# Loading queries and keys 20 steps ahead of their pair instead of 11, in a bucketed attention kernel with a routed expert layer

## The chip, the core and the metric

The kernel runs on one core of one Trainium2 chip. TensorE (PE, with its weight loads shown apart as PEld), VectorE (DVE), ScalarE (ACT) and GpSimd (POOL) compute; SyncE (SP) issues nearly all the DMAs and computes nothing. The metric is the device time of one execution in microseconds, as the median of several runs. A profiled execution gives the span between its first and last instruction, and the trace that is read here.

## What is computed

There are 4 batches of 8 heads, 768 positions of 64 numbers each, and then 8 experts over 3072 tokens of 512 numbers. Cut to what matters:

```python
q_bits = (q @ proj > 0);  k_bits = (k @ proj > 0)          # 6 bits for each position and head
mask = bucket(q_bits)[:, None] == bucket(k_bits)[None, :]
scores = where(mask, q @ k.T / 8, -1e9)
attn = exp(scores - max); attn /= attn.sum() + 1e-9
x = (attn @ v) laid out as 3072 tokens x 512
e = argmax(x @ w_gate);  out = gate * eom * (relu(x @ w1[e]) @ w2[e])
```

## The kernel before

The attention half goes over 16 pairs of heads (`g` from 0 to 15). A pair is 12 steps of scores, 192 steps in all, and a step is one tile of 128 queries against 768 keys for one head. The kernel writes out by hand what PE, DVE, ACT and POOL do in each step, in program order, so these four follow the code. SP is not among them: its DMAs are put in order by the framework that builds the program, which starts from the step where they stand in the code, and SP then works through that order, waiting at each DMA until its source is there and its target free.

Within a step `s`: `scores(s)` multiplies on PE (L533) and DVE copies the result with the mask's limit and the minimum (L537); `soft` is the exponential on ACT (L545); `normal` scales two steps' rows by their reciprocal sums on POOL (L555); `transposed(s - 6)` turns the tile of six steps earlier on PE (L566), and ACT copies it out (L567). At every sixth step from step 12 on there is a longer block: under "matmuls" stands `weighted`, 12 products with the values of six steps (24 matmuls of PE, L577).

What the change touches is how a pair is made ready:

- `load(g)`, L393 to L399: two DMAs of 384 KB, one for each head, bring queries and keys into tiles `qk`. There are 4 such tiles, so pair `g` takes those of pair `g - 2`.
- `project(g)`, L405 to L416: 8 small matmuls (L411), four for each head, and one DVE operation (L414) give the sign bits `bt` of the hash.
- `split_hi` and `split_lo`, L485 to L500: POOL and DVE make two float32r parts of `qk`, in tiles `xl` and `yl`.
- `spread(g, j)`, L502 to L516: for each head 8 DMAs of SP from one place of the on-chip memory to another put these parts and the bits into the form that `scores` reads.
- `load_v(g)` (L401 to L403) brings the values of a pair, `rows` (L582 to L596) writes a finished pair to memory in four DMAs.

The loop over `g` near L721 gives these functions their steps. With `s0 = 12 * (g - 1)`, which is the first step of the pair before, the kernel has: `load(g)` at step `s0 - 11`, at the end of it; `project(g)` in the block of step `s0 - 6`, behind `weighted`; splits and spreads of pair `g` in the block of step `s0`. Scores of pair `g` begin at step `s0 + 12`. `plan(step, fn)` puts a function at the end of a step, `block(step, when, fn)` at a named place inside a long block. Loads of pairs 0 and 1 stand ahead of the loop over steps, and pair 1 has steps of its own.

After the attention follow the routing of tokens to experts and the expert layer, whose weights are loaded by SP as well. None of their code is touched.

Of the kernel before, what the change touches and what calls it, by code (L numbers as in the profile page):

```python
# [45 lines left out]
PER = 6  # L46
# [13 lines left out]
def lsh_attention_then_moe(  # L60
# [307 lines left out]
    with ExitStack() as actx:  # L368
# [16 lines left out]
        def plan(step, *fns):  # L385
            at.setdefault(step, []).extend(fns)

        def block(step, when, *fns):

            around.setdefault((step, when), []).extend(fns)  # L390


        def load(g, heads=(0, 1)):  # L393
            st = pairs[g]
            st.setdefault("qk", [])
            for j in heads:
                t = hp.tile([P, S], F32, name="qk", bufs=4)
                nc.sync.dma_start(t, qkT[2 * g + j])
                st["qk"].append(t)  # L399

        def load_v(g):  # L401
            pairs[g]["v"] = tp.tile([P, 2, NT, D], F32, name="vt", bufs=2)
            nc.sync.dma_start(pairs[g]["v"], v[g])  # L403

        def project(g):  # L405
            st = pairs[g]
            pp = ps_m.tile([P, HS], F32, name="ps_m")
            for j in range(2):
                for n in range(2):
                    r = 32 * (2 * j + n)  # L410
                    nc.tensor.matmul(pp[r:r + 32], pjc, st["qk"][j][:, n * HS:(n + 1) * HS],  # L411
                                     start=True, stop=True)
            bt = hp.tile([P, HS], F32R, name="bt", bufs=2)
            nc.vector.tensor_scalar(bt, pp, thr, scl, ALU.is_gt, ALU.mult)  # L414
            st["bt"] = bt
# [69 lines left out]
        def split_hi(g, j, xl=None):  # L485
            st = pairs[g]
            for k in ("xl", "yl", "xr", "yr"):
                st.setdefault(k, [None, None])
            if xl is None:
                xl = hp.tile([P, S], F32R, name="xl")  # L490
            nc.gpsimd.tensor_scalar(xl, st["qk"][j], sgn, 0.0, ALU.mult, ALU.add)
            st["xl"][j] = xl

        def split_lo(g, j, n):
            st = pairs[g]
            if n == 0:
                st["yl"][j] = hp.tile([P, S], F32R, name="yl")
            cs = slice(n * HS, (n + 1) * HS)
            nc.vector.scalar_tensor_tensor(st["yl"][j][:, cs], st["qk"][j][:, cs], sgn, f32(st["xl"][j][:, cs]),
                                           ALU.mult, ALU.subtract)  # L500

        def spread(g, j):  # L502
            st = pairs[g]
            xl, yl, bt = f32(st["xl"][j]), f32(st["yl"][j]), f32(st["bt"])
            st["xr"][j] = hp.tile([P, S], F32R, name="xr")
            st["yr"][j] = hp.tile([D + 2 * NB, S], F32R, name="yr")
            xr, yr = f32(st["xr"][j]), f32(st["yr"][j])
            nc.sync.dma_start(xr[0:D], xl[D:P])
            nc.sync.dma_start(yr[0:D], xl[D:P])
            nc.sync.dma_start(xr[D:P], yl[D:P])  # L510
            nc.sync.dma_start(xl[D:P], xl[0:D])
            for n in range(2):
                r = 32 * (2 * j + n)
                cs = slice(n * HS, (n + 1) * HS)
                nc.sync.dma_start(yr[D:D + 2 * NB, cs], bt[r + 2 * NB:r + 4 * NB])
                nc.sync.dma_start(yl[D:D + 2 * NB, cs], bt[r:r + 2 * NB])  # L516
# [52 lines left out]
        def weighted(hb, c):  # L569
            g, hf = hb // 2, hb % 2  # L570
            st = pairs[g]
            if c == 0:
                st["av"] = ps_a.tile([P, HS], F32, name="ps_a")
            if c == NT - 1 and hf == 0:
                st["ot"] = gp.tile([P, S], F32, name="ot", bufs=4)
            for j in range(2):
                nc.tensor.matmul(st["av"][j * D:(j + 1) * D], st["v"][:, j, c], blocks[hb][j][:, c],  # L577
                                 start=(c == 0), stop=(c == NT - 1))
            if c == NT - 1:
                nc.vector.tensor_copy(st["ot"][:, hf * HS:(hf + 1) * HS], st["av"])  # L580

        def rows(g, hf, whole=True):  # L582

            b, i = divmod(g, H // 2)
            st = pairs[g]
            if hf == 0:
                st["xb"] = gp.tile([P, S // 32, 32], F32, name="xb", bufs=2)
            ts = slice(hf * HS // 32, (hf + 1) * HS // 32)
            nc.vector.transpose(st["xb"][:, ts].rearrange("p n c -> p (n c)"), st["ot"][:, hf * HS:(hf + 1) * HS])
            if whole:  # L590
                if hf == 0:
                    return
                ts = slice(0, S // 32)
            xv = x_dram[b * S:(b + 1) * S].rearrange("(n r) c -> r n c", r=32)
            for a in range(4):
                nc.sync.dma_start(xv[:, ts, i * P + 32 * a:i * P + 32 * (a + 1)], st["xb"][32 * a:32 * (a + 1), ts])  # L596
# [124 lines left out]
        for g in range(NP):  # L721
            s0 = 12 * (g - 1)
            if g >= 2:
                plan(s0 - 11, lambda g=g: load(g))
                block(s0 - PER, "matmuls", lambda g=g: project(g))
                block(s0, "head", *(lambda g=g, j=j: split_hi(g, j) for j in range(2)))
                block(s0, "early", lambda g=g: split_lo(g, 0, 0))
                block(s0, "amid", lambda g=g: split_lo(g, 0, 1), lambda g=g: split_lo(g, 1, 0))
                block(s0, "behind", lambda g=g: split_lo(g, 1, 1), *(lambda g=g, j=j: spread(g, j) for j in range(2)))
            elif g == 1:  # L730
                plan(4, lambda: project(1))
                for j in range(2):
                    plan(2 + j, lambda j=j: split_hi(1, j))
                    for n in range(2):
                        plan(3 + 2 * j + n, lambda j=j, n=n: split_lo(1, j, n))
                    plan(5 + j, lambda j=j: spread(1, j))
            if g >= 1:
                plan(s0 + 10, lambda g=g: load_v(g))
            for hf in range(2 if g + 1 < NP else 1):
                block(12 * g + 6 * hf + 2 * PER, "matmuls", *(  # L740
                    lambda hb=2 * g + hf, c=c: weighted(hb, c) for c in range(NT)))
                if g + 1 < NP:
                    plan(12 * g + 6 * hf + 2 * PER, lambda g=g, hf=hf: rows(g, hf))
        for i, fn in enumerate(more_constants()):
            plan(18 + 2 * i, fn)
        for b in range(B - 1):
            r = routing(b)
            s0 = 12 * (H // 2) * (b + 1)
# [10 lines left out]
        s0 = 12 * (NP - 1)  # L759
# [415 lines left out]
```

## Time and profile before

| | us |
|---|---|
| median of 3 runs | 780.19 (777.91 to 780.93) |
| the profiled execution | 777.2 |
| its span, first to last instruction | 775.5 |
| PE busy | 750.9, 97% of the span |
| DVE, ACT, POOL busy | 483.2, 460.9, 387.7 |
| PE idle in 0 to 530 us while waiting for `qk` | 7.8 in 9 waits |

The profiled execution is the one that all rows come from, so sums are made against its own 777.2. Matmuls overlap on PE: a timeline row's duration may reach into the next row, and what a group of matmuls costs is best read as the distance from its start to the start of the group behind it. A step of the attention half is some 2.2 us long on average, a pair some 26 us.

### The profile page before, as it was taken

To read this page: it belongs to the slowest core of one execution; us is meant where nothing else is said; L and a number is where in the kernel's file an instruction comes from. 1 tells how busy PE (TensorE), PEld (TensorE's weight loads), DVE (VectorE), ACT (ScalarE), POOL (GpSimd) and SP (SyncE) were. 2 spreads that over 40 slices of the span, in tenths; PEclk is the share of its full clock that TensorE was granted. 3 is DMA by queue.
4 is the path that set the end of the run, shared out by engine and by line. 5 is a ranking of instruction groups with operands and counts; after the bars stand their busy time and mean duration, and the time that the engine had idled before them with its cause. 6 is when DMAs were issued, how large, how long until landed. Compare 5 with 4: busy or idle time off the path is not lost. (4 is left out here: it accounts for less than half of the span.)

```text
span 775.5 us, 13677 instructions
## 1 busy us (share of the span) xinstructions
PE 750.9 (97%) x4690; PEld 607.9 (78%) x4690; DVE 483.2 (62%) x1032; ACT 460.9 (59%) x934; POOL 387.7 (50%) x422
## 2 busy tenths in 40 slices
PE   7899989999999999999999999999999999999997
PEld 5667766867767677686778768988999999989895
DVE  5757756788766787676798727246263635455540
ACT  5768868778777877788787841243342534353331
POOL 7545635445553554555357893453537363736201
PEclk9999999999999999999999999999999999999999
DMA  4564464555455555554545332363444444446501
GB/s 169 116 173 98 88 167 110 107 132 135 99 140 116 108 128 121 141 116 106 117 89 151 77 93 68 122 214 118 144 153 155 152 150 155 151 151 218 195 18 39
DMA packets 84799, 98.89 MB, mean 128 GB/s; under 512 B 57999, under 2 KB 59439, under 8 KB 84720
## 3 DMA queue, kind: packets, MB, share of 16 engines
q1 hardware_dynamic: 79376, 84.58, 42.2%
q0 software_dynamic: 5200, 13.31, 5.1%
q8 instruction: 40, 0.66, 0.3%
q14 instruction: 39, 0.32, 0.1%
q10 hardware_dynamic: 144, 0.02, 0.0%
HBM read 59.49 MB, written 13.11 MB: 94 GB/s over the span
## 5 line engine op out<-in xcount | busy, mean ns | idle before, releaser
L555 POOL TENSOR_SCALAR sc<-sc,rsum 128x768 f32<-128x768 f32 x192 | 185.9, 982 | 202.7 <-DVE rsum L553 99.4
L567 ACT COPY pts<-ps_t 128x384 f32<-128x384 f32 x384 | 165.1, 483 | 93.4 <-PE ps_t L566 92.4
L537 DVE TENSOR_SCALAR_CACHE_REDUCE sc<-ps_s 128x768 f32<-128x768 f32 x192 | 182.6, 954 | 55.7 <-PE ps_s L533 53.0
L545 ACT ACTIVATE sc<-sc,mn 128x768 f32<-128x768 f32 x192 | 178.2, 935 | 7.7 <-DVE sc L537 7.7
L566 PE MATMUL ps_t<-ident,sc 128*128 128x128 f32 x1152 | 160.7, 275 | 3.3 <-ACT pts L567 2.9
L566 PEld LDWEIGHTS ps_t<-ident,sc 128*128 128x128 f32 x1152 | 133.5, 141 | 33.5 <-POOL sc L555 16.2
L577 PE MATMUL ps_a<-pts,vt 128*64 128x384 f32 x768 | 131.1, 491 | 0.0
L533 PE MATMUL ps_s<-xr,xl 128*128 128x384 f32 x384 | 115.3, 382 | 3.6 <-POOL xl L481 2.2
L577 PEld LDWEIGHTS ps_a<-pts,vt 128*64 128x64 f32 x768 | 52.2, 137 | 67.7 <-issue 67.5
L323 DVE SCALAR_TENSOR_TENSOR hl<-ps_s,hh 128x256 fp32r<-128x256 f32 (+8 forms) x40 | 34.0, 849 | 108.0 <-ACT hh L322 108.0
L533 PE MATMUL ps_s<-yr,yl 76*128 76x384 f32 x384 | 99.8, 341 | 0.6 <-POOL yr L443 0.5
L312 PE MATMUL ps_s<-xh,w1h 128*128 128x256 f32 (+7 forms) x288 | 97.1, 337 | 1.7 <-DVE eq L647 1.6
L312 PE MATMUL ps_s<-xlo,w1h 128*128 128x256 f32 (+7 forms) x288 | 95.4, 331 | 0.0
L312 PE MATMUL ps_s<-xh,w1l 128*128 128x256 f32 (+7 forms) x288 | 95.2, 331 | 0.0
L286 POOL DMA_INDIRECT xq<-x_dram,idx x75 | 82.7, 1102 | 23.7 <-issue 20.8
L329 POOL DMA_INDIRECT out_dram<-yo,sid x29 | 30.6, 1056 | 115.8 <-ACT yo L328 63.9
L322 ACT ACTIVATE hh<-ps_s 128x256 fp32r<-128x256 f32 (+8 forms) x40 | 29.0, 726 | 96.6 <-PE ps_s L312 96.6
L533 PEld LDWEIGHTS ps_s<-yr,yl 76*128 76x128 f32 x384 | 70.5, 191 | 1.2 <-POOL yr L443 1.2
L533 PEld LDWEIGHTS ps_s<-xr,xl 128*128 128x128 f32 x384 | 58.7, 193 | 6.5 <-POOL xl L481 2.5
L312 PEld LDWEIGHTS ps_s<-xh,w1h 128*128 128x128 f32 x288 | 54.2, 188 | 3.8 <-issue 2.4
L312 PEld LDWEIGHTS ps_s<-xlo,w1h 128*128 128x128 f32 x288 | 54.2, 188 | 1.3 <-DVE xlo L269 0.2
L312 PEld LDWEIGHTS ps_s<-xh,w1l 128*128 128x128 f32 x288 | 54.1, 188 | 1.1
(204 smaller groups left out, 1024.4 us busy)
## 6 DMA issues: line engine op xcount, KB each, us to landing
w_raw<-in_w_dram SPq DMA_DIRECT2D x36, 512.0 KB
qk<-in_qkT_dram SPq DMA_DIRECT2D x32, 384.0 KB
xh<-in_w_dram SPq DMA_DIRECT2D x14, 512.0 KB
xlo<-in_w_dram SPq DMA_DIRECT2D x14, 512.0 KB
vt<-in_v_dram SPq DMA_DIRECT2D x16, 384.0 KB
xr<-xl SPq DMA_DIRECT2D x30, 192.0 KB
yr<-xl SPq DMA_DIRECT2D x30, 192.0 KB
xr<-yl SPq DMA_DIRECT2D x30, 192.0 KB
```

What stands on the lines that cost most here:

```text
L286: nc.gpsimd.indirect_dma_start(out=xq[:, k * P:(k + 1) * P], out_offset=None, in_=x_dram.rearrange("n (a f) -> (n a) f", a=NB32), in_offse ...
L312: nc.tensor.matmul(ps, l, r, start=first and k == 0, stop=last and k == len(pairs) - 1)
L322: nc.scalar.activation(hh, ph, AF.Relu)
L323: return lambda: nc.vector.scalar_tensor_tensor(hl, ph, 0.0, f32(hh), ALU.max, ALU.subtract)
L329: nc.gpsimd.indirect_dma_start(out=out[:, :], out_offset=bass.IndirectOffsetOnAxis(ap=sid[0:n, r, a:a + 1], axis=0), in_=yo[0:n], in_offse ...
L533: nc.tensor.matmul(ss[:, n, 0:HS], l[0:k, qs], r[0:k, n * HS:(n + 1) * HS], start=first, stop=not first)
L537: nc.vector.tensor_scalar(sc, ss[:, :, 0:HS], MASKED, None, ALU.min, ALU.min, accum_out=mn)
L545: nc.scalar.activation(pr, pr, AF.Exp, bias=mn, scale=-1.0, accum_out=sums[s // GROUP][:, k:k + 1])
L555: nc.gpsimd.tensor_scalar(live[s0 + k], live[s0 + k], rs[:, k:k + 1], 0.0, ALU.mult, ALU.add)
L566: nc.tensor.transpose(tr[:, c], pr[:, (3 * h + c) * P:(3 * h + c + 1) * P], ident)
L567: nc.scalar.copy(pts[:, 3 * h:3 * h + 3, t * P:(t + 1) * P], tr)
L577: nc.tensor.matmul(st["av"][j * D:(j + 1) * D], st["v"][:, j, c], blocks[hb][j][:, c], start=(c == 0), stop=(c == NT - 1))
```

## The change

Three numbers change in the loop that gives the steps. From pair 3 on, `load(g)` stands at step `s0 - 20`, not `s0 - 11`, which is four steps behind the block in which pair `g - 2` is split and spread (for pair 3 at step 8, not 13). For pair 2 the load stays at step 1, and its projection goes from the block of step 6 to the end of step 10. Nothing is added or taken away.

```diff
             if g >= 2:
-                plan(s0 - 11, lambda g=g: load(g))
-                block(s0 - PER, "matmuls", lambda g=g: project(g))
+                plan(max(s0 - 20, 8) if g > 2 else 1, lambda g=g: load(g))
+                if g > 2:
+                    block(s0 - PER, "matmuls", lambda g=g: project(g))
+                else:
+                    plan(10, lambda g=g: project(g))
                 block(s0, "head", *(lambda g=g, j=j: split_hi(g, j) for j in range(2)))
```

On SP, the stretch between the spreads of two pairs, before. The first row is the last DMA of the spread of pair 4; `qk_1264` and `qk_1266` are pair 5, `qk_1605` and `qk_1607` pair 6; the last row opens the spread of pair 5:

```order
L516 DMA yl_1180<-bt_1027 12x384
L398 DMA qk_1264<-in_qkT_dram 128x768
L398 DMA qk_1266<-in_qkT_dram 128x768
L403 DMA vt_1484<-in_v_dram 128x768
L398 DMA qk_1605<-in_qkT_dram 128x768
L398 DMA qk_1607<-in_qkT_dram 128x768
L596 DMA x_dram_63<-xb_1239 32x24x32 x4
L508 DMA xr_1551<-xl_1512 64x768
```

The same stretch now. The first row is again the last DMA of the spread of pair 4, `qk_1327` and `qk_1329` are pair 6, and the last row opens the spread of pair 5:

```order
L516 DMA yl_1184<-bt_1031 12x384
L398 DMA qk_1327<-in_qkT_dram 128x768
L398 DMA qk_1329<-in_qkT_dram 128x768
L596 DMA x_dram_63<-xb_1243 32x24x32 x4
L403 DMA vt_1488<-in_v_dram 128x768
L508 DMA xr_1555<-xl_1516 64x768
```

Pair 5's loads have moved ahead of the spread of pair 4, out of this stretch; what stands behind that spread is the load of pair 6 alone, and the values now come behind the rows that are written out. Before, such stretches held by turns anything from no load to four (two pairs' worth); now each holds one pair's two.

On SP near the start, before, around the spread of pair 2 (it runs from `xr_495` to the last `bt_326`; `qk_549` and `qk_551` are pair 3):

```order
L516 DMA yl_305<-bt_283 12x384
L508 DMA xr_495<-xl_456 64x768
L509 DMA yr_496<-xl_456 64x768
L510 DMA xr_495<-yl_463 64x768
...
L516 DMA yl_470<-bt_326 12x384
L398 DMA qk_549<-in_qkT_dram 128x768
L398 DMA qk_551<-in_qkT_dram 128x768
```

And now (`qk_381` and `qk_383` are pair 3, `qk_612` pair 4):

```order
L516 DMA yl_305<-bt_283 12x384
L398 DMA qk_381<-in_qkT_dram 128x768
L398 DMA qk_383<-in_qkT_dram 128x768
L508 DMA xr_499<-xl_460 64x768
L509 DMA yr_500<-xl_460 64x768
...
L516 DMA yl_474<-bt_432 12x384
L398 DMA qk_612<-in_qkT_dram 128x768
```

Pair 3's load stood behind the spread of pair 2 and now stands ahead of it.

On PE the only move is pair 2's projection. Before, at step 6 (`sc_198` is the tile of step 0):

```order
L411 MATMUL ps_m_321<-qk_225,pjc_66 32x384 x2
L411 MATMUL ps_m_321<-qk_227,pjc_66 32x384 x2
L566 MATMUL ps_t_330<-ident_68,sc_198 128x128 x3
L566 MATMUL ps_t_335<-ident_68,sc_198 128x128 x3
L533 MATMUL ps_s_351<-xr_154,xl_150 128x384 x2
```

And now, at the end of step 10 (`sc_269` is the tile of step 4):

```order
L566 MATMUL ps_t_415<-ident_68,sc_269 128x128 x3
L566 MATMUL ps_t_420<-ident_68,sc_269 128x128 x3
L411 MATMUL ps_m_427<-qk_225,pjc_66 32x384 x2
L411 MATMUL ps_m_427<-qk_227,pjc_66 32x384 x2
L533 MATMUL ps_s_434<-xr_154,xl_150 128x384 x2
```

The 8 matmuls (a row counts a pair of them as one) stand four steps later, and the DVE operation L414 on their result moves with them. Every other instruction of PE, DVE, ACT and POOL keeps its place.

## Rows read from the trace of the kernel before

**Rows 1.** The page: busy time by engine, and the clock that TensorE was granted in 40 slices of the span (9 is nine tenths or more of full speed).

```profile
PE 750.9 (97%) x4690; PEld 607.9 (78%) x4690; DVE 483.2 (62%) x1032; ACT 460.9 (59%) x934; POOL 387.7 (50%) x422
...
PEclk9999999999999999999999999999999999999999
```

**Rows 2.** Who waited for whom, of PE alone, from 0 to 530 us: microseconds in total, times, longest.

```profile
PE ps_m L411 <- DMA qk<-in_qkT_dram: 7.8, 9, 1.7
PE ps_t L566 <- ACT pts L567: 2.9, 4, 1.9
```

**Rows 3.** Timeline of PE around the projection of pair 5: start, duration, and in brackets the idle time ahead of it with what ended that.

```profile
100.66 4.09 PE L577 MATMUL ps_a<-pts,vt 128*64 128x384 f32 x24
106.50 0.84 PE L411 MATMUL ps_m<-qk,pjc 128*32 128x384 f32 x4 [1.75 <-DMA qk<-in_qkT_dram]
108.38 0.84 PE L411 MATMUL ps_m<-qk,pjc 128*32 128x384 f32 x4 [1.04 <-DMA qk<-in_qkT_dram]
109.15 0.88 PE L566 MATMUL ps_t<-ident,sc 128*128 128x128 f32 x6
...
116.72 0.60 PE L533 MATMUL ps_s<-xr,xl 128*128 128x384 f32 x2
```

**Rows 4.** Timeline of PE around the projection of pair 4.

```profile
74.93 4.09 PE L577 MATMUL ps_a<-pts,vt 128*64 128x384 f32 x24
78.95 0.85 PE L411 MATMUL ps_m<-qk,pjc 128*32 128x384 f32 x8
79.73 0.88 PE L566 MATMUL ps_t<-ident,sc 128*128 128x128 f32 x6
```

**Rows 5.** Timeline of PE around the projections of pairs 3, 7, 9, 11, 13 and 15, two rows for each: for pair 3 the group ahead of the projection and the one behind it, for the others the first half of the projection and the group behind its second half.

```profile
46.41 4.09 PE L577 MATMUL ps_a<-pts,vt 128*64 128x384 f32 x24
...
54.03 0.87 PE L566 MATMUL ps_t<-ident,sc 128*128 128x128 f32 x6
...
161.74 0.84 PE L411 MATMUL ps_m<-qk,pjc 128*32 128x384 f32 x4
...
163.55 0.87 PE L566 MATMUL ps_t<-ident,sc 128*128 128x128 f32 x6
...
215.86 0.84 PE L411 MATMUL ps_m<-qk,pjc 128*32 128x384 f32 x4
...
218.60 0.87 PE L566 MATMUL ps_t<-ident,sc 128*128 128x128 f32 x6
...
271.18 0.84 PE L411 MATMUL ps_m<-qk,pjc 128*32 128x384 f32 x4
...
273.06 0.88 PE L566 MATMUL ps_t<-ident,sc 128*128 128x128 f32 x6
...
325.40 0.84 PE L411 MATMUL ps_m<-qk,pjc 128*32 128x384 f32 x4
...
327.87 0.88 PE L566 MATMUL ps_t<-ident,sc 128*128 128x128 f32 x6
...
380.46 0.84 PE L411 MATMUL ps_m<-qk,pjc 128*32 128x384 f32 x4
...
382.66 0.87 PE L566 MATMUL ps_t<-ident,sc 128*128 128x128 f32 x6
```

**Rows 6.** Timeline of SP's DMA queue: when the DMA instructions were issued. The row at 48.15 is the last of the spread of pair 2, the one at 53.36 the load of pair 4; the one at 103.07, right behind the spread of pair 4, is the load of pair 5, and the one at 105.16 that of pair 6.

```profile
48.15 0.71 SPq L516 DMA_DIRECT2D yl<-bt  x1
...
53.36 0.98 SPq L398 DMA_DIRECT2D qk<-in_qkT_dram  x2
...
103.07 0.98 SPq L398 DMA_DIRECT2D qk<-in_qkT_dram  x2
...
105.16 0.91 SPq L398 DMA_DIRECT2D qk<-in_qkT_dram  x2
110.46 2.13 SPq L596 DMA_DIRECT2D x_dram<-xb  x4
```

**Rows 7.** Busy time of each engine in three stretches: length, busy time and instructions of PE, PEld, DVE, ACT and POOL, granted clock of PE, DMA share and GB/s. The first runs from the end of `weighted` to the transposes behind the projection of pair 5, the other two are the 12 steps behind it and the 12 behind those (each up to the end of the next projection, without its wait).

```profile
104.68:109.15 4.47, 1.68 (x11) 0.29 (x9) 0.77 (x3) 0.50 (x2) 1.91 (x3) 1.00 0.87 280
...
109.15:135.64 26.49, 26.49 (x186) 19.24 (x184) 18.71 (x45) 21.50 (x49) 12.67 (x14) 1.00 0.52 119
135.64:162.52 26.88, 26.88 (x190) 19.91 (x186) 20.76 (x56) 21.78 (x51) 12.46 (x13) 1.00 0.54 117
```

**Rows 8.** Timeline of POOL in the block of pair 5's projection: the scalings whose results the transposes behind it read.

```profile
103.02 1.78 POOL L555 TENSOR_SCALAR sc<-sc,rsum 128x768 f32<-128x768 f32 x2 [3.24 <-DVE rsum L553]
105.22 1.78 POOL L555 TENSOR_SCALAR sc<-sc,rsum 128x768 f32<-128x768 f32 x2 [0.41 <-ACT sc L545]
```

**Rows 9.** The start, where pair 2's projection stands: timeline of PE, then one row of ACT's, then one stretch of 2 us with the columns of rows 7.

```profile
20.84 0.85 PE L411 MATMUL ps_m<-qk,pjc 128*32 128x384 f32 x8
...
25.49 1.51 PE L566 MATMUL ps_t<-ident,sc 128*128 128x128 f32 x6 [1.95 <-ACT pts L567]
...
28.08 1.00 PE L566 MATMUL ps_t<-ident,sc 128*128 128x128 f32 x6
...
24.89 0.84 ACT L567 COPY pts<-ps_t 128x384 f32<-128x384 f32 x2
...
26.00:28.00 2.00, 2.00 (x9) 1.99 (x8) 0.55 (x2) 0.96 (x2) 0.45 (x1) 0.50 0.18 40
```

**Rows 10.** The first scores of pair 2 at step 24, on PE.

```profile
61.60 0.60 PE L533 MATMUL ps_s<-xr,xl 128*128 128x384 f32 x2
```

## The prediction

> **What bounds the kernel now.** I read the page's busy times first: PE is busy 97% of the span and the next engine 62%, at full granted clock in all 40 slices [rows 1]. So PE's order of work sets the end, and what can be won without removing work is PE's idle time. Next the waits of PE in the attention half: the largest by far is the projection (L411) waiting for the load of queries and keys, 7.8 us in 9 waits [rows 2]. Then I looked at the timeline of PE around single projections. In pair 5, `weighted` starts at 100.66, the first half of the projection comes only at 106.50, its second half at 108.38, and the transposes behind it at 109.15 [rows 3]. In pair 4 the same stretch has no gap: 74.93, 78.95, 79.73 [rows 4]. The reader is to see that every other pair looks like rows 3 and the rest like rows 4. The DMA queue says why. Pair 5's load was issued at 103.07, behind the whole spread of pair 4, while PE wanted it near 104.7; pair 6's load followed at 105.16, most of a period ahead of its need [rows 6]. Odd pairs are late, even ones early. Outside the waits PE has no slack: the 12 steps after pair 5's late projection, 26.49 us, and the next 12, 26.88 us, are filled by PE to the last hundredth [rows 7].
>
> **The term that counts: seven late loads.** What a wait costs is more than its idle time: the late projection runs as two halves that follow each other, where the early one runs its eight matmuls in one go. I therefore take start distances. From rows 4, `weighted` takes 78.95 - 74.93 = 4.02 and a projection without a wait 79.73 - 78.95 = 0.78.
> - Pair 3: 54.03 - (46.41 + 4.02) - 0.78 = 2.82 [rows 5].
> - Pair 5: 109.15 - (100.66 + 4.02) - 0.78 = 3.69 [rows 3].
> - Pairs 7, 9, 11, 13, 15, where only the second half is late: from the first half's start to the next transposes 1.81, 2.74, 1.88, 2.47, 2.20, each less 0.78: 1.03, 1.96, 1.10, 1.69, 1.42 [rows 5].
>
> The sum is 13.71 us. The lower bound is the bare idle time, 7.8 [rows 2]: that is what would be won if halves still ran apart. I take 13.71, because the seven pairs would then have what rows 4 show, eight matmuls in a row whose data has long been there.
>
> **Does the load come early enough?** In the new order SP issues a pair's load right behind the spread of the pair two before it, so a period (26 us) earlier than before. Pair 5's load would then go out not at 103.07 but near 103.07 - 26 = 77, behind the spread of pair 3. From issue to use the late load of rows 3 and 6 took 106.50 - 103.07 = 3.4 us for the first half and at most 108.38 - 103.07 = 5.3 us for both; 26 us hold that many times over. Nor does the load wait for its tile: tile `qk` of pair `g - 2` is read last by that pair's `split_lo` and `split_hi`, and the spread that stands ahead of the load on SP waits for the same results. Behind the load on SP stand the rows to be written and the values. The rows wait for a step six further on, so the load's issue, 0.98 us for two [rows 6], fits before it. The values now stand behind the rows; they serve a `weighted` some 14 steps later, more than 30 us, which covers a shift of the few us between them.
>
> **What is late next, where the wait goes.** The transposes behind the projection read POOL's scaled tiles. In pair 5's block the first scaling pair is done at 103.02 + 1.78 = 104.80 and the second at 107.00 [rows 8]. Without the wait the first transposes would start at 109.15 - 3.69 = 105.46, 0.66 us behind that, and no tile of the second pair is wanted before the third step. ACT has no wait to offer either: only 2.9 us of PE's waits in this half come from it [rows 2], and in 26.49 us it is busy for 21.50 [rows 7]. If the 0.66 us were gone, the price is whatever POOL is behind, in each of seven places.
>
> **Pair 2's projection, from step 6 to step 10.** At step 6 it costs PE 0.78 us of a stretch in which PE then stands idle for 1.95 us until ACT has copied a tile out (25.49) [rows 9]. ACT's copy follows its exponentials, which do not read the projection, so PE comes to 25.49 no sooner without it. At step 10 PE is dense, and there it costs its 0.78. So +0.78 is taken. Below that, 0 if some wait remains at step 10. Above it, the clock: after the idle time PE ran at granted clock 0.50, which is 1.2 GHz, and from 25.49 to 28.08 spent 2.59 us on what takes about half of that at 2.4 GHz [rows 9]. With less work at step 6 the slow stretch could begin earlier or last longer, by at most another such stretch: +1.3. So 0 to 2.1. The load of pair 3 issued ahead of pair 2's spread costs PE nothing as long as that spread ends in time (rival 3).
>
> **A rule on the clock.** In the wait of pair 5 PE was busy 1.68 of 4.47 us and the granted clock stayed 1.00, and it was 1.00 in the 12 steps behind [rows 7]; so no term for the clock is in the 13.71. The Trainium skill, "TensorE: Matmul & The Clock Gate", Part 1, says that the array's clock falls to half when PE has been idle and comes back with activity. By that rule the waits could have cost extra time that now comes back, and the quiet stretch at the start, which loses a projection, could cost more. The first half is not borne out by these rows; the second is the upper end of the term above, and the sum by it would be 1.3 us higher.
>
> **Sum.** 777.2 - 13.71 + 0.78 = 764.3 for an execution like the profiled one. That one lies 3.0 under the median of the runs, 780.19, so I apply the difference, -12.9, to the median: 767.3.
>
> **Rivals.**
> 1. *Smaller gain: only the idle time comes back.* The halves still run apart, or POOL's 0.66 us of margin is eaten. 777.2 - 7.8 + 0.78 = 770.2, at the median 773.2. For it: the margin is thin. Against it: the even pairs have the same blocks and no such loss [rows 4]. 10%.
> 2. *No change: the load is not issued earlier in fact.* If its tile came free a period later than I think, the load would stand where it stood, and hold the rows and values behind it. -0 + 0.78: 778.0, at the median 781.0. Against it: the order on SP puts the spread that needs the same splits ahead of it. 6%.
> 3. *Slower: loads delay spreads.* Every stretch of the queue now carries a load directly behind a spread, and once, for pair 3, ahead of one. A spread that lands late stalls the scores of its pair. Pair 2's spread ended its issue at 48.15 + 0.71 = 48.86 [rows 6]; its scores start at 61.60 [rows 10], which becomes 61.60 - 2.82 + 0.78 = 59.56, so 10.7 us lie between. The load ahead of it adds 0.98 of issue and at most the 5.3 us of transfer: 4.4 remain. In later pairs, say 4, the spread ends at 103.07 [rows 6] and the scores start at 116.72 - 3.69 = 113.03 [rows 3], 10.0 us. PE stalls from the point where a spread lands more than 10 us after its last issue, by the excess, in each of up to 13 pairs; to end slower takes 12.9 / 13 = 1.0 us in each. At 1.4 us in each, 18.2 in all: 777.2 - 12.9 + 18.2 = 782.5, at the median 785.5. Nothing in rows 6 takes so long. The Trainium skill, "DMA: Bandwidth & Descriptors", section on queues, rings and completion order, says that each DMA engine takes the descriptors of one issuing engine's queue in the order of issue. That speaks against this change at one place: pair 2's spread waits behind 768 KB. By that rule the delay is the 5.3 us already counted, and the sum stays. 5%.
>
> **How the numbers follow.** My forecast, waits gone, 764.3 (767.3 at the median), 79%. Its own range: the runs of before lie from 2.3 below their median to 0.7 above it, and the start costs from 0.8 less to 1.3 more: 764.2 to 769.3. The range given takes in rival 1, 773.2, to the full, and leaves out rivals 2 and 3, 11%, with some loss at either edge: 763.5 to 773.5. What a measurement of this kernel can tell from no change is about 0.5%, 3.9 us. Faster by more than that: forecast and rival 1, less a little for a half-gain between rivals 1 and 2, 0.87. Within it: rival 2 and that half-gain, 0.08. Slower: 0.05.
>
> **What would show it.** In the profile after, no projection from pair 3 on should have an idle time that ends with a load of `qk`; all should be one row of eight matmuls of 0.85 with the transposes 0.78 behind its start. The list of PE's waits should lose its 7.8. Twelve steps should take 25.7 to 26.9 us everywhere. The attention half should end 12 to 13 us earlier and the expert half be as long as before. Pair 2's projection should stand near 31 us with 0.78 and nothing else of note; a longer stretch at clock 0.50 near 26 us shows the upper end. The forecast is wrong if the transposes behind a projection wait for POOL (rival 1), if SP's loads are issued a period later than said (rival 2), or if the first scores of a pair wait for the DMAs of a spread (rival 3).

## The result, and the profile after

| | before | changed |
|---|---|---|
| median, us | 779.05 (4 runs, 776.78 to 780.93) | 766.03 (4 runs, 765.09 to 766.78) |
| ratio | | 0.9834, 95% interval 0.9801 to 0.9866 |
| the profiled execution | 777.2 | 766.78 |
| its span | 775.5 | 765.0 |

The change saves 13.0 us at the median, and 10.5 us between the two profiled executions. The two need an explanation each. First the profile after, against [rows 1]:

```profile
PE 746.3 (98%) x4690; PEld 608.2 (80%) x4690; DVE 481.5 (63%) x1032; ACT 461.1 (60%) x934; POOL 387.8 (51%) x422
...
PEclk9799999999999999999999999999999999999999
```

PE is fuller than before, and one slice near the start now has a granted clock of 0.7. PE's waits from 0 to 520 us (total, times, longest), against [rows 2]:

```profile
PE ps_s L533 <- DVE sc L537: 2.6, 1, 2.6
PE ps_s L533 <- POOL xl L481: 2.2, 1, 2.2
PE ps_t L566 <- POOL sc L555: 1.6, 2, 1.3
...
PE ps_m L678 <- DVE bt L414: 1.0, 3, 0.3
```

The 7.8 us of waiting for `qk` are gone altogether, and no wait for a spread has come. The first three rows lie in the start, before step 12, but for 0.33 us of the third at 440. The last is new. Around the projection of pair 5 [rows 3] PE's timeline is now:

```profile
99.42 4.09 PE L577 MATMUL ps_a<-pts,vt 128*64 128x384 f32 x24
103.45 0.85 PE L411 MATMUL ps_m<-qk,pjc 128*32 128x384 f32 x8
104.23 0.88 PE L566 MATMUL ps_t<-ident,sc 128*128 128x128 f32 x6
```

That is, row by row, what pair 4 showed [rows 4]: 4.03 from `weighted` to the projection, 0.78 to the transposes, no bracket. SP in the stretch behind the spread of pair 4 (issue, duration, count), against [rows 6]:

```profile
101.89 0.99 SPq L398 DMA_DIRECT2D qk<-in_qkT_dram  x2
105.56 2.13 SPq L596 DMA_DIRECT2D x_dram<-xb  x4
107.80 0.49 SPq L403 DMA_DIRECT2D vt<-in_v_dram  x1
```

Each such stretch now has one pair's load, and PE uses this one, pair 6's, only at 129.95. Finally windows, with the columns of [rows 7]; the first holds the 12 steps behind pair 5's projection up to just before the next projection (129.95), the others belong to the start [rows 9]:

```profile
104.23:129.80 25.57, 25.57 (x180) 19.08 (x176) 18.20 (x45) 21.27 (x48) 13.33 (x15) 1.00 0.55 123
...
24.00:26.00 2.00, 0.73 (x4) 0.36 (x3) 1.73 (x7) 1.77 (x4) 1.46 (x2) 0.50 0.33 96
26.00:28.00 2.00, 2.00 (x10) 2.00 (x9) 0.00 (x0) 0.96 (x2) 0.55 (x1) 0.50 0.12 25
28.00:30.00 2.00, 2.00 (x10) 1.90 (x9) 0.96 (x2) 0.70 (x2) 0.00 (x0) 0.55 0.95 195
```

The 12 steps are full of PE. With the next projection they end at 130.73 and take 130.73 - 104.23 = 26.50 us, against 26.49 before [rows 7], so outside the waits nothing got shorter. The half clock at the start lasts longer than before: from 28 to 30 us the granted clock is 0.55, where it was 0.89.

**Where the 10.5 us went, place by place.** I take the start of the transposes behind each odd pair's projection, after less before. Pair 3: 52.80 - 54.03 = -1.23. Pair 5: 104.23 - 109.15 = -4.92, so 3.69 more, as forecast. Pair 7: 157.61 - 163.55 = -5.94, 1.02 more. Pair 9: 211.07 - 218.60 = -7.53, so only 1.59 more where 1.96 was due. Pair 15: 371.32 - 382.66 = -11.34. Two things stand against the seven gains. At pair 3 the changed kernel was 1.6 us behind its due: `weighted` of step 12 came at 35.53, not at 33.94. And behind pairs 7, 11 and 15 about 0.37 us is given back each time. So the attention half, up to the first product of the experts (L312), ends 444.38 - 455.44 = -11.06 us earlier. PE at these two places, before and after:

```profile
33.94 4.09 PE L577 MATMUL ps_a<-pts,vt 128*64 128x384 f32 x24
...
455.44 0.36 PE L312 MATMUL ps_s<-xh,w1h 128*128 128x256 f32 x1
```

```profile
35.53 4.09 PE L577 MATMUL ps_a<-pts,vt 128*64 128x384 f32 x24
...
444.38 0.36 PE L312 MATMUL ps_s<-xh,w1h 128*128 128x256 f32 x1
```

With 0.5 us more in the expert half that makes: -13.71 + 1.6 + 3 x 0.37 + 0.5 = -10.5. The expert half is the same code in all twelve profiles of this document and takes from 319.5 to 321.9 us in them, so those 0.5 us lie within its scatter.

The 0.37 us is the new wait. PE after, behind the projection of pair 7:

```profile
156.83 0.85 PE L411 MATMUL ps_m<-qk,pjc 128*32 128x384 f32 x8
157.61 0.88 PE L566 MATMUL ps_t<-ident,sc 128*128 128x128 f32 x6
158.83 0.18 PE L678 MATMUL ps_m<-ohb,tri 128*128 128x48 bf16 x1 [0.34 <-DVE bt L414]
...
159.00 0.59 PE L533 MATMUL ps_s<-xr,xl 128*128 128x384 f32 x2
```

DVE after, in the same stretch:

```profile
157.66 0.54 DVE L580 COPY ot<-ps_a 128x384 f32<-128x384 f32 x1
158.11 0.67 DVE L414 TENSOR_SCALAR bt<-ps_m,pj 128x384 fp32r<-128x384 f32 x1
```

L678 is the first product of `prefix`, a step of the routing that runs once for each of the first three batches, at the end of a step whose block holds a projection (pairs 7, 11, 15). It writes to a tile `ps_m`, of which there is one, and the projection's result stands in it until DVE has made `bt` (L414) of it. Before, the same place read, PE and then DVE:

```profile
163.55 0.87 PE L566 MATMUL ps_t<-ident,sc 128*128 128x128 f32 x6
164.40 0.18 PE L678 MATMUL ps_m<-ohb,tri 128*128 128x48 bf16 x1
...
164.58 0.60 PE L533 MATMUL ps_s<-xr,xl 128*128 128x384 f32 x2
```

```profile
163.67 0.68 DVE L414 TENSOR_SCALAR bt<-ps_m,pj 128x384 fp32r<-128x384 f32 x1 [0.57 <-DMA qk<-in_qkT_dram]
```

From the transposes to the scores 1.03 us before, 1.39 after. While PE waited for the load, DVE worked off its queue and then stood idle for 0.57 us, so L414 could start right behind the projection, 0.12 us behind the start of the transposes. Without the wait DVE is still at its copy (L580) and comes to L414 0.50 us behind it. The late load had hidden a queue on DVE.

### The profile page after: what moved, and what is told of

The parts are those of the page before. It is cut to its first block, busy times and chain, and to the rows that moved or that the text cites. A ratio compares the mean times of both kernels' runs of the same rounds, so it can differ in the third digit from the quotient of the medians.

```text
span 765.0 us, 13703 instructions
## 1 busy us (share of the span) xinstructions
PE 746.3 (98%) x4690; PEld 608.2 (80%) x4690; DVE 481.5 (63%) x1032; ACT 461.1 (60%) x934; POOL 387.8 (51%) x422
## 5 line engine op out<-in xcount | busy, mean ns | idle before, releaser
L312 PE MATMUL ps_s<-xh,w1h 128*128 128x256 f32 (+7 forms) x288 | 97.0, 337 | 1.5 <-DVE eq L647 1.4
L312 PE MATMUL ps_s<-xlo,w1h 128*128 128x256 f32 (+7 forms) x288 | 95.3, 331 | 0.0
L312 PE MATMUL ps_s<-xh,w1l 128*128 128x256 f32 (+7 forms) x288 | 95.2, 331 | 0.0
L312 PEld LDWEIGHTS ps_s<-xh,w1h 128*128 128x128 f32 x288 | 54.2, 188 | 3.6 <-issue 2.2
L312 PEld LDWEIGHTS ps_s<-xh,w1l 128*128 128x128 f32 x288 | 54.1, 188 | 1.4 <-DVE w1l L178 0.3
L312 PEld LDWEIGHTS ps_s<-xlo,w1h 128*128 128x128 f32 x288 | 54.1, 188 | 1.3 <-DVE xlo L269 0.2
```

The costliest lines, as they stand in the source:

```text
L312: nc.tensor.matmul(ps, l, r, start=first and k == 0, stop=last and k == len(pairs) - 1)
```

## The experiments

Four ran beside one another, then four, then two; the medians of the kernel before were 779.21, 778.29 and 779.53 beside them.

**1. The changed kernel again.** No edit.

> The changed kernel as it is, for the size of the gain in one job. Theory 1 (seven late loads gone, 13.7 us, less 1.4 at the start and 1.1 in three new waits of the prefix matmul for bt) expects 10.5 to 11.5 us less than the kernel before of the same job, in median and in the profile. The rival (something beyond PE's waits, such as the quieter queue, gives another 2 us) expects the 13.0 that the two medians so far differ by.

766.95 us (765.52 to 769.13), ratio 0.9836 (0.9808 to 0.9863), profiled span 765.0. No wait for `qk`, again three waits of L678 for L414, 1.0 us in all, and `weighted` of step 12 at 35.30. What the first profile showed is not a single draw. The gain is 12.3 us at the median, between the 10.5 to 11.5 of the theory and the 13.0 of its rival, so the medians decide for neither.

**2. The loads alone: pair 2's projection back in the block of step 6.** Against the changed kernel:

```diff
-                if g > 2:
-                    block(s0 - PER, "matmuls", lambda g=g: project(g))
-                else:
-                    plan(10, lambda g=g: project(g))
+                block(s0 - PER, "matmuls", lambda g=g: project(g))
```

> Loads as in the changed kernel, pair 2's projection back in the block of step 6. Theory (the move costs 0.78 us of dense PE plus some 0.6 us of half clock at the start): weighted of step 12 starts 1.3 to 1.6 us earlier than in the changed kernel (35.5 there), the seven late loads stay away, whole kernel 1.4 us under the changed one. Rival (the move costs nothing, the difference at the start is chance): start and time as in the changed kernel within 0.3 us in the profile. Second rival (the early load of pair 3 needs the projection out of the way): a wait for qk or a spread near 20 to 60 us.

764.66 us (764.32 to 766.71), ratio 0.9812 (0.9782 to 0.9841), 2.3 us under the changed kernel; no wait for `qk`. The loads are the whole gain, and the move of pair 2's projection takes some of it away. PE at the start of this kernel, and one window:

```profile
21.67 1.51 PE L411 MATMUL ps_m<-qk,pjc 128*32 128x384 f32 x8
...
32.92 4.09 PE L577 MATMUL ps_a<-pts,vt 128*64 128x384 f32 x24
```

```profile
26.00:28.00 2.00, 2.00 (x17) 1.96 (x17) 1.48 (x4) 1.19 (x4) 0.84 (x1) 1.00 0.17 36
```

Step 12's `weighted` starts 2.4 to 2.6 us earlier than in the two profiles of the changed kernel, and the window 26 to 28 has granted clock 1.00, where the changed kernel had 0.50. Both differences are larger than the theory said (1.3 to 1.6 us at the start, 1.4 in all).

**3. The other half alone: only pair 2's projection moved.** Against the kernel before:

```diff
-                block(s0 - PER, "matmuls", lambda g=g: project(g))
+                if g > 2:
+                    block(s0 - PER, "matmuls", lambda g=g: project(g))
+                else:
+                    plan(10, lambda g=g: project(g))
```

> Loads as in the kernel before, only pair 2's projection at the end of step 10. Theory: all seven waits stay (13.7 us), the start is 0.8 to 2.4 us longer, the whole kernel the same as before or up to 2 us slower. Rival (the move is a part of the gain, by giving the start room): 1 us or more faster than the kernel before.

776.89 us (774.88 to 779.33), ratio 0.998 (0.9962 to 0.9998). The waits for `qk` stay, 5.8 us in 9. The start is late here too (step 12 at 35.68, 1.74 behind the first profile of the kernel before), yet the end isn't: the transposes behind pair 5's projection stand at 109.18, where they stood at 109.15. The loads land when they land, so what the start loses there the shorter waits give back: the seven late projections cost 11.8 us, not 13.7. The price of this move shows only once the loads are early. By the times this went against the theory: the kernel is 1.4 us faster than the one before at the median, as the rival said, and the interval just excludes no change. The two profiled spans are equal (775.5), so where that comes from stays open; with the loads early the move is a loss (experiment 2).

**4. The waits removed in another way: the projections later, the loads as before.** Against the kernel before:

```diff
-                block(s0 - PER, "matmuls", lambda g=g: project(g))
+                if g > 2:
+                    plan(s0 - 3, lambda g=g: project(g))
+                else:
+                    block(s0 - PER, "matmuls", lambda g=g: project(g))
```

> Loads at step s0 - 11 as before; instead, from pair 3 on the projection stands three steps later (end of step s0 - 3). If the gain is PE no longer waiting for a load, whoever moves, no projection waits for qk here either, and with pair 2 at step 6 and no prefix behind a projection the time is 13.7 us under the kernel before, 2 to 3 under the changed one. If the gain needs the loads a period earlier (a calmer queue, spreads landing sooner), it stays near the kernel before, with less than half of the gain. If three steps are too short for the load, waits for qk remain, at most 5 us in all.

767.93 us (767.41 to 768.81), ratio 0.9849 (0.9821 to 0.9878). No wait for `qk` is left, and the gain, 11.3 us, is nearly that of experiment 1. So it does not need the loads a period earlier: pair 5's load is issued at 99.76 here, behind the spread of pair 4 as before, and its projection stands at 106.27. The edit was not as clean as meant: SP's order changed with it, to one pair's load in each stretch. A calmer queue as the cause is ruled out not by this run but by the steps outside the waits, which are as long with either order (26.49 and 26.50 above). The time is 1.0 us above the changed kernel, where 2 to 3 below was expected. It pays more at the single `ps_m` tile, by PE's timeline:

```profile
186.05 0.85 PE L411 MATMUL ps_m<-qk,pjc 128*32 128x384 f32 x8
187.83 1.58 PE L226 MATMUL ps_m<-t_rhs,t_ob 128*128 128x96 f32 x12 [0.93 <-DVE bt L414]
```

Another product of the routing now stands right behind the projection and waits 0.93 us for L414, twice in all, and the prefix product waits 1.1 us once for DVE.

**5. The new wait taken away: the prefix product one step later.** Against the changed kernel:

```diff
-                          (15, r["best"]), (18, r["prefix"]), (20, r["ranks"]), (22, r["places"]),
+                          (15, r["best"]), (19, r["prefix"]), (20, r["ranks"]), (22, r["places"]),
```

> The changed kernel with the prefix matmuls of the routing one step later (19, not 18, behind a batch's start). Theory (without the wait for the load, the prefix matmul stands 0.3 us too close behind the projection, waiting for DVE's bt in the one ps_m tile): the three waits of 0.33 us are gone, 1.0 to 1.1 us less in the attention half of the profile. Rival (the wait moves on to ranks or to the transposes): no gain, and a wait of the same length one step later. In the times either is at the edge of what they tell.

764.55 us (763.96 to 767.8), ratio 0.9814 (0.9786 to 0.9843), 2.4 under the changed kernel beside it. PE's timeline:

```profile
155.06 0.85 PE L411 MATMUL ps_m<-qk,pjc 128*32 128x384 f32 x8
157.92 0.19 PE L678 MATMUL ps_m<-ohb,tri 128*128 128x48 bf16 x1
...
181.12 0.85 PE L411 MATMUL ps_m<-qk,pjc 128*32 128x384 f32 x8
```

The waits of L678 are gone. From projection to projection it is 181.12 - 155.06 = 26.06 us, against 183.38 - 156.83 = 26.55 in the changed kernel: 0.49 less. From `weighted` of step 12 to the first product of the experts it is 441.22 - 33.75 = 407.47, against 444.38 - 35.53 = 408.85: 1.4 less for the three places, where 1.0 to 1.1 was expected. The rest of the earlier end is the start, which is no effect of this edit: the code up to step 12 is the changed kernel's, but `weighted` came at 33.75 in this execution and at 35.53 and 35.30 in those. How much of the 2.4 at the median is the edit is therefore open.

**6. The kernel before, again.** No edit.

> The kernel before once more, for a second profile of it. The seven late projections should cost 13.7 us again within 1 (the waits are set by the order on SP, not by chance). The start up to the weighted of step 12, which came at 33.9 in the first profile and between 32.9 and 35.5 in the runs since, should differ by up to 1.5 us if its clock is a matter of chance, and the same if it follows the code.

777.76 us (774.98 to 779.02), ratio 0.9988 (0.9974 to 1.0002). One thing differs from the first profile. PE around the projection of pair 3, and windows there:

```profile
45.28 4.09 PE L577 MATMUL ps_a<-pts,vt 128*64 128x384 f32 x24
52.69 2.71 PE L411 MATMUL ps_m<-qk,pjc 128*32 128x384 f32 x8 [3.32 <-DMA qk<-in_qkT_dram]
55.33 1.54 PE L566 MATMUL ps_t<-ident,sc 128*128 128x128 f32 x6
```

```profile
49.30:52.00 2.70, 0.07 (x2) 0.00 (x0) 0.78 (x3) 0.51 (x2) 2.21 (x5) 0.94 0.58 164
52.00:54.00 2.00, 1.31 (x6) 0.29 (x8) 0.00 (x0) 0.00 (x0) 0.72 (x3) 0.50 0.96 334
...
56.00:58.00 2.00, 2.00 (x10) 1.90 (x9) 0.61 (x2) 0.96 (x2) 0.00 (x0) 0.50 0.45 126
```

PE came 1.1 us earlier to pair 3 and met one wait of 3.32 us, after which it ran at 1.2 GHz, and still did in the window that ends at 58. This wait cost 55.33 - 45.28 - 4.02 - 0.78 = 5.25 us, not 2.82. Being later by then, pair 5 lost less, 110.84 - 103.45 - 4.80 = 2.59, not 3.69. All seven came to 14.2, within 1 of 13.7 as expected, without what the half clock cost in the steps behind. The start came at 32.82, not 33.94, so for one code it does differ by 1.1.

**7. How much earlier is enough: the load at `s0 - 13`.** Against the kernel before:

```diff
-                plan(s0 - 11, lambda g=g: load(g))
+                plan(s0 - 13 if g > 2 else 1, lambda g=g: load(g))
```

> From pair 3 on the load at step s0 - 13, one step ahead of the block with the spread of the pair before, so that on SP every load stands directly ahead of a spread and not behind one; pair 2's projection at step 6, as before. Theory: no projection waits for qk, time as project2_back, 764 to 766. Rival (768 KB ahead of a spread in SP's queue delay it by some 5 us and the scores of a pair then wait for it): waits of the first scores of a pair for spread DMAs, 1 us or more in each of 13 pairs, over 778.

764.63 us (763.78 to 765.41), ratio 0.9827 (0.9806 to 0.9849). SP behind the spread of pair 4 (its end is the first row), and the projection of pair 5 on PE:

```profile
98.28 0.71 SPq L516 DMA_DIRECT2D yl<-bt  x1
102.70 2.14 SPq L596 DMA_DIRECT2D x_dram<-xb  x4
104.95 0.49 SPq L403 DMA_DIRECT2D vt<-in_v_dram  x1
105.48 1.16 SPq L398 DMA_DIRECT2D qk<-in_qkT_dram  x2
109.95 0.53 SPq L508 DMA_DIRECT2D xr<-xl  x1
```

```profile
96.57 4.09 PE L577 MATMUL ps_a<-pts,vt 128*64 128x384 f32 x24
100.59 0.85 PE L411 MATMUL ps_m<-qk,pjc 128*32 128x384 f32 x8
```

Every load stands last in its stretch, directly ahead of a spread (L508): the place where rival 3 saw danger, in every pair. No scores wait for a spread and no projection for a load. Two steps of code do what nine did.

**8. The same in the other direction: the load at `s0 - 9`.** Against the kernel before:

```diff
-                plan(s0 - 11, lambda g=g: load(g))
+                plan(s0 - 9 if g > 2 else 1, lambda g=g: load(g))
```

> The kernel before with one number changed: from pair 3 on the load stands two steps later in the code, at s0 - 9 and not at s0 - 11. The order on SP stays in the main what it was: by turns a stretch with the loads of two pairs behind a spread, and one with none. If that order sets the waits, as the prediction argued, the time is that of the kernel before, 776 to 781, and PE's waits for queries and keys again come to 6 to 9 us, at the odd pairs. If the step in the code sets them, each load is about two steps or 4.4 us later: the odd pairs lose 4.4 us more in seven places, some 30 us, and the time is near 808.

778.92 us (777.65 to 780.0), ratio 0.9992 (0.9972 to 1.0011). PE's waits, the projection of pair 3, and SP behind the spread of pair 4:

```profile
PE ps_m L411 <- DMA qk<-in_qkT_dram: 8.5, 8, 3.1
```

```profile
52.23 3.00 PE L411 MATMUL ps_m<-qk,pjc 128*32 128x384 f32 x8 [3.08 <-DMA qk<-in_qkT_dram]
```

```profile
104.24 0.99 SPq L398 DMA_DIRECT2D qk<-in_qkT_dram  x2
105.92 0.33 SPq L403 DMA_DIRECT2D vt<-in_v_dram  x1
106.30 0.91 SPq L398 DMA_DIRECT2D qk<-in_qkT_dram  x2
110.59 2.26 SPq L596 DMA_DIRECT2D x_dram<-xb  x4
```

The pattern of [rows 6], two pairs' loads in one stretch, and the time of before. The step in the code does not count by itself: two steps later cost nothing, two earlier won everything. What counts is between which spreads SP has the load.

**9. Loads 20 ahead, pair 2's projection at step 6, the prefix product one step later.** Edits 2 and 5 together; against the kernel before:

```diff
-                plan(s0 - 11, lambda g=g: load(g))
+                plan(max(s0 - 20, 8) if g > 2 else 1, lambda g=g: load(g))
...
-                          (15, r["best"]), (18, r["prefix"]), (20, r["ranks"]), (22, r["places"]),
+                          (15, r["best"]), (19, r["prefix"]), (20, r["ranks"]), (22, r["places"]),
```

> Loads 20 steps ahead as in the changed kernel, pair 2's projection back at step 6, prefix one step later: the two costs that the runs showed are both taken out. If they add up, 1.3 us under project2_back in the profile and 2 to 3 under the changed kernel, median 763 to 764.5. If they do not (something else, such as the gathered rows at step 182, comes late instead), the profile equals the better of project2_back and prefix_later.

762.39 us (761.86 to 763.54), ratio 0.9798 (0.9778 to 0.9817). The best of the versions at the median, ahead of both kernels and a little under the 763 to 764.5 expected. No wait of L678 remains; step 12 at 33.23. The two edits add up: from there to the first product of the experts it takes 440.75 - 33.23 = 407.52, as in experiment 5, from a start nearly as early as in experiment 2. The largest entry of PE's waits from 0 to 520 us:

```profile
PE ps_t L566 <- ACT pts L567: 3.0, 4, 2.0
```

**10. The same with the load at `s0 - 13`.** Edits 7 and 5 together; against experiment 9:

```diff
-                plan(max(s0 - 20, 8) if g > 2 else 1, lambda g=g: load(g))
+                plan(s0 - 13 if g > 2 else 1, lambda g=g: load(g))
```

> The load of pair g two steps earlier than before, at s0 - 13, pair 2's projection where it was, and the prefix product one step later (+19). If the late loads and the three waits of the prefix product for the sign bits are the two independent costs, this gives what the version with loads 20 ahead and both other edits gave, 761 to 764, without any wait of L678 for L414. If the longer lead of the loads is itself worth something, it stays 1 us or more above that version's 762.4.

764.17 us (763.44 to 766.66), ratio 0.9806 (0.9762 to 0.985). No wait of L678 for L414. By the ratio it is level with experiment 9. By the medians it is 1.8 above, of which 1.2 is how the kernel before ran beside each. The attention half ends no later: the first expert product (L312) starts at 439.72, in experiment 9 at 440.75; that the span is longer all the same (761.6 against 760.6) comes from the expert half, which no load of `qk` touches. So the longer lead of the loads is worth nothing that could be shown.

## Why the prediction was right, and where its sizes were off

- **Seven late loads**: right, in mechanism and size. Pairs 5 and 7 gave 3.69 and 1.02, against 3.69 and 1.03, and all projections are one row of eight. Rival 1 falls, and with it the lower bound of 7.8. The term is not a constant of the kernel, though: pair 3's loss was 2.82 in one execution and 5.25 in another (experiment 6), and 5.31 in experiment 8, where PE also came early and met one wait of 3.08.
- **Early enough**: right. The load behind the spread of pair 3 was issued at 76.61, where near 77 was forecast. Rival 2 falls. That the order on SP is the cause, and not the step, is shown by experiments 7 and 8 together.
- **What is late next**: this is the step of the prediction that failed. It looked at POOL and ACT and found no wait. POOL's margin of 0.66 us did hold, but DVE was not asked about. Behind pairs 7, 11 and 15 the prefix product waits for L414: 3 x 0.37 = 1.1 us by the distances between the two kernels, 1.4 us by experiment 5. It was readable before: at 163.67 DVE's idle time ended with the same load that PE had waited for, and at 0.57 it was shorter than the 1.03 that would go. The difference, 0.46, is how late L414 would be, less what margin L678 had, which started at 164.40, just behind its end at 163.67 + 0.68.
- **Pair 2's projection**: right in sign, mis-sized. Of 0.78, with bounds of 0 and 2.1, the upper one was right. With the projection at step 6, eight executions start step 12's `weighted` at 32.44 to 33.94, mean 33.0; with it at step 10, four start it at 33.75 to 35.68, mean 35.1. That is 2.1 us, and experiment 2 gives 2.3 at the median. 0.78 of it is the projection among dense work; the rest goes with the half clock, which filled 26 to 28 in the changed kernel and most of 28 to 30 (0.55), and was gone from 26 on in experiment 2 (1.00). In experiment 5, with the projection at step 10 but clock 1.00 from 26 on, the start came at 33.75, just 0.75 behind the mean of 33.0. That the move makes the half clock last is likely, not shown: three of the four had 0.50 from 26 to 28, and of the eight only the first profile. The prediction's full clock in all 40 slices hid this, since a slice of [rows 1] is 19.4 us long.
- **A rule on the clock**: the prediction said of the Trainium skill, "TensorE: Matmul & The Clock Gate", Part 1, that its first half, time lost to the clock behind the waits, is not borne out. One more execution of the same kernel bears it out: after 3.32 us of waiting the granted clock was 0.50, and pair 4's projection stood at 81.75, 26.42 us behind pair 3's transposes, against 78.95 - 54.03 = 24.92 in the first profile. Experiment 8 had it too, with 0.50 from 52 to 54 us behind a wait of 3.08. The waits at pair 5 in the first profile, of 1.75 and 1.04 us, left it at 1.00 [rows 7].
- **Sum and median**: the median came out 1.3 us under the forecast because two errors nearly cancel, which is luck. The profiled execution came to 766.78, 2.5 above the forecast 764.3: 0.8 for the start, 1.1 for the new wait, 0.5 in the expert half. The attention half ended 11.1 us earlier, where 12 to 13 was forecast. But the step from execution to median was wrong the other way. Before, the profiled execution lay 3.0 under the median of the runs shown; after, it lies 0.75 above. I had scaled the 3.0 on as if it belonged to the method.
- **What stays open** is where those 3.0 us were. The first profile of the kernel before seems to have lost less than others do. From `weighted` of step 12 to the first expert product it took 455.44 - 33.94 = 421.50 us. In experiment 6, the same kernel, it was 456.26 - 32.82 = 423.44, and in experiment 8, with the waits as before, 456.10 - 32.59 = 423.51; in both PE started earlier, met one long wait at pair 3 and had clock 0.50 behind it. In the changed kernel it took 408.85, and 408.81 in experiment 1. With 2.1 for the start this gives an estimate of 423.5 - 408.8 - 2.1 = 12.6 us for the gain, near the 13.0 and 12.3 of the medians. How many executions have the long wait is not known, and the two profiled ones that had it took 777.61 and 779.24, no more than the medians of the kernel before beside them (778.29 and 779.53). The 45 executions of the kernel before beside the experiments have spans from 774.0 to 782.0: the eleven with a mean granted clock of 0.990 or less have a mean span of 778.8, the sixteen at 0.994 or more one of 776.2. The six of the changed kernel in experiment 1 lie within 3.6 us, at 0.990 to 0.992, but the ten of experiment 8, which keeps the waits, lie within 2.3 us. Only profiled executions show where the clock fell, and none of the longest ones was profiled. So that the long waits make the scatter is argued, not shown, and experiment 8 speaks against it.
- **Rival 3**: falls, since no scores waited for a spread in the changed kernel, nor in experiment 7, with the load directly ahead of each spread.

## What to carry to other kernels

When a wait is removed, ask of every engine what it did in that time, not only of those that feed the waiting one: an engine that used the wait to work off its queue can be late afterwards, and a product that shares a single tile with the work just made punctual can show it. For a DMA whose place is set by a scheduler, look at the neighbours in its queue, since the step in the code may move by two without any effect, or by two and win everything. A difference between one profiled execution and the median is not a property to scale on as long as it is not known what makes the executions scatter.

## What was not expected of the hardware

- The same kernel took its projection of pair 3 at full clock in one execution, behind waits of 1.51 and 0.41 us, and at 0.50 in another, whose wait there was 3.32 us. The projection behind it took 2.71 us and not 0.85.
- An idle time of 1.95 us ahead of the transposes near 25.5 us was followed by granted clock 0.50 from 26 to 28 in the first profile of the kernel before, and by 1.00 in experiment 8, where it was as long.
- The start is not the same each time: for one code up to step 12, `weighted` came at 33.75, 35.30 and 35.53. In the first of these PE's window 26 to 28 had clock 1.00, in the last 0.50:

```profile
26.00:28.00 2.00, 2.00 (x18) 1.97 (x16) 0.69 (x1) 1.23 (x3) 0.59 (x1) 1.00 0.13 28
```

That row is the kernel of experiment 5. A change of 2 us at the start of this kernel can therefore not be read from one profile.
